# Expert blocks of four chunks on one resident x, and chunk states updated in pairs

## The chip, the cores and the metric

The kernel runs on one core of a Trainium2 chip. The metric is the time of one execution in microseconds of device time, as the median of several runs; one further execution was profiled, and all rows below come from it. Engines are named as in the profile: PE is TensorE, PEld its weight loads, DVE VectorE, ACT ScalarE, POOL GpSimd, SP the queue that issues the DMAs.

## The reference, cut to what matters

A gated linear attention (4 batches, 8 heads, 768 positions, head size 40) feeds a bilinear expert layer (3072 tokens, 320 to 1536 to 320).

```python
for t in range(S):                                   # per batch and head
    m_new = maximum(f_gate[t] + m, i_gate[t])
    f_stab, i_stab = exp(f_gate[t] + m - m_new), exp(i_gate[t] - m_new)
    C = f_stab * C + i_stab * outer(v[t], k[t])
    n = f_stab * n + i_stab * k[t]
    y[t] = sigmoid(o_gate[t]) * (C @ q[t]) / maximum(abs(n @ q[t]), 1)
x = y.transpose(0, 2, 1, 3).reshape(3072, 320)
out = ((x @ w_a) * (x @ w_b)) @ w_out
```

## The kernel before, in words

**Chunks.** The attention is computed in 24 chunks of 128 positions of one batch, in the order of `chunks`: chunk n belongs to batch n % 4 and to position group c = n // 4. A chunk's state (C and n, eight heads) goes to the chunk four places later. The chunk's stages are generators: `stage_e` (decay table `gbc`), `stage_a` (q and k split into bf16 parts `qks` and transposed into `T` by DMA), `stage_v` (v split), `stage_b` (scores, `pS`), `stage_i` (what the state gives, `pI`), `stage_c` (scores times v, `pV`, and the weighted v `vw` for the state), `stage_u` (state update: `pU`, `cst`, its bf16 split `cb`), `stage_f` (denominator and output gate, result y in `osig`) and `stage_d` (y transposed by PE into `pX`, then split into a high part `xh` and a low part `xl`: the expert layer's x). `put_state` and `get_state` carry the split state through device memory (`c_dram`) into the layout `cx` in which `stage_i` reads it. Chunks 0 to 5 take float32 forms (`begin_*`), the later ones bf16 splits. q, k and v lie in a ring of three chunks.

**Blocks.** `moe_block` runs the expert layer over a block of chunks: `sizes` is 2, 2, 3, 3, 3, 3, 3, 2, 3. For each of 12 slices of 128 hidden columns, `up` does two groups of 8 matmuls with the weights as stationary and x (256 or 384 columns) as moving operand into a PSUM bank `pu` each; the first group is copied out (`g`), the second multiplied with it (`g` again, on DVE), and the product is split into `gh` and `gl`; `down`, two slices behind (`LAG = 2`), does three matmuls of 320 columns for each chunk into the chunk's bank `pd`. After the last slice each `pd` is copied to `o` and stored.

**Order.** While block kb runs on the experts, the attention of block kb+1 runs beside it (`run_block`). Everything is first recorded in a `Plan`, which links the recorded nodes by their data and buffers, gives each a cost (`cost`), and settles by list scheduling in `TURNS` tries which engine does a free choice (`copier`: ACT or DVE; `adder`: DVE or POOL) and in which order each engine's and SP's in-order queue runs (`settle`). So all instructions are recorded with the same helper line, and the groups below are told apart by their tiles.

**Memory.** PSUM's eight banks are three for `pu` (shared with the early stages), three for `pd` and two for the attention (`ps_at`). `xh` and `xl` exist twice, so a block's x is written while the block before reads its own. Weights are converted early from 64-bit inputs through a ring `cv` of four buffers, which later takes the output tiles `o`.

Of the kernel before, what the change touches and what calls it, by code (L numbers as in the profile page):

```python
# [20 lines left out]
PSUM = bass.MemoryType.PSUM  # L21
TURNS = 40
TRIALS = 4
# [71 lines left out]
class Root:  # L95

    def __init__(self, make, ring, ndim, shape):
        self.make, self.tile, self.ring = make, None, ring
        self.full = tuple((0, n) for n in shape)
        self.first, self.users = None, []  # L100

# [6 lines left out]
class Node:  # L108
    __slots__ = ("i", "eng", "alts", "calls", "by", "prev", "next", "table", "acc", "wide", "use", "pair", "least")

    def __init__(self, i, alts):
        self.i, self.alts, self.eng = i, alts, alts[0]
        self.calls, self.prev, self.next, self.acc = [], {}, [], []
        self.by = {e: [0.0, 0.0, 0.0, False] for e in alts}
        self.table, self.wide, self.use = None, True, 0.0


class Plan:
# [20 lines left out]
    def add(self, engines, op, args, kw):  # L139
# [3 lines left out]
        acc = []  # L143
        for j, x in enumerate(refs):
            key, box = self.where(x)
            if key is not None:
                acc.append((key, box, j == 0))
                if j == 0 and op == "matmul" and not kw.get("start", True):
                    acc.append((key, box, False))
# [3 lines left out]
        if not (  # L153
            alts[0] == "PE" and node is not None and node.eng == "PE" and len(node.calls) < 8
            and (node.acc[0][0] == okey or self.pair and node.pair)
        ):
# [24 lines left out]
    def cost(self, node, by, eng, op, out, refs, args, kw):  # L181
# [5 lines left out]
        if eng == "PE":  # L187
            if op == "transpose":
                occ = 0.109
            else:  # L190
# [12 lines left out]
            by[1] = 0.17  # L203
            plain = size[1] == 4 and op == "matmul" and "float32r" not in f32[0]
            node.use += cols * refs[1].shape[0] * (1 + plain) / 128.0 * out.shape[0] / 128.0
# [78 lines left out]
    def run(self, rank, forward=True, fixed=None, odds=None):  # L284
# [17 lines left out]
        other = {"DVE": "POOL", "POOL": "DVE"}  # L302
        order, count, filling = [], 0, False

# [53 lines left out]
        while count < len(nodes):  # L358
# [56 lines left out]
            if e == "PE" and forward:  # L415
# [6 lines left out]
                while filling and fixed is None:  # L422
# [130 lines left out]
def kernel(  # L553
# [20 lines left out]
    DV = D + 2  # L574
    TB = 3
    NTB = TB * P
    WCH = 384
    CVB = 4
    STAGES = 8
# [18 lines left out]
    ps_at = tile_pool("ps_at", 2, PSUM)  # L598


    ident = wpool.tile([P, P], F32, name="ident")
# [15 lines left out]

    cst = [wpool.tile([P, HH, DV], F32, name=f"cst{b}") for b in range(B)]
    cxp = [[wpool.tile([P, H, DV], BF16, name=f"cx{b}_{w}") for w in range(2)] for b in range(B)]
# [34 lines left out]
    NCH = len(chunks)  # L654
    sizes = [2, 2, 3, 3, 3, 3, 3, 2, 3]
    NB = len(sizes)
# [380 lines left out]
    def stage_c(n):  # L1037
# [4 lines left out]
        if c < NC - 1:  # L1042
            vw = apool.tile([P, H, DV], F32, tag="vw", name=f"vw{n}", bufs=1)
            nc.gpsimd.tensor_tensor(
# [20 lines left out]

    def stage_u(n):
        c, b = chunks[n]
        if c == NC - 1:
            return
        s = st[n]  # L1070
# [4 lines left out]
        pu = pU[:, 0:HH * DV].rearrange("p (h d) -> p h d", h=HH)  # L1075
        for h in range(H):
            r, _, x = half(h)
            nc.tensor.matmul(
                pu[r:r + 64, x], nat(n)[0][:, 1, h, :], s["vw"][:, h], start=True, stop=True
            )  # L1080
        t = cst[b]
        if c == 0:
            nc.scalar.copy(t, pu)
        else:
            nc.vector.tensor_tensor(
                t, t, dec[:, c - 1, b * HH:(b + 1) * HH].unsqueeze(2).broadcast_to([P, HH, DV]),
                op=ALU.mult,
            )
            nc.vector.tensor_tensor(t, pu, t, op=ALU.add)
        yield  # L1090
        if n + B < NF32:
            return
        cb = apool.tile([P, 3, HH, DV], BF16, tag="cb", name=f"cb{n}", bufs=1)
        cr = apool.tile([P, H * DV], F32, tag="tmp", name=f"cr{n}")[:, 0:HH * DV]
        cr = cr.rearrange("t (h d) -> t h d", h=HH)
        nc.scalar.copy(cb[:, 2], t)
        nc.gpsimd.tensor_tensor(cr, t, cb[:, 2], op=ALU.subtract)
        yield
        if n < 8:
            nc.scalar.copy(cb[:, 1], cr)  # L1100
        else:
            nc.vector.tensor_copy(cb[:, 1], cr)
        nc.gpsimd.tensor_tensor(cb[:, 0], cr, cb[:, 1], op=ALU.subtract)
        states[n] = cb
        yield

# [42 lines left out]

    xt = {}  # L1150

    def stage_d(n):
        s = st[n] if n < NS else st.pop(n)
        k_ = block[n]
        t0 = (n - begins[k_]) * P
        if t0 == 0:
            xt[k_] = (
                mpool.tile([P, 3, NTB], F32R, tag="xh", name=f"xh{k_}", bufs=2),
                mpool.tile([P, 3, NTB], F32R, tag="xl", name=f"xl{k_}", bufs=2),
            )  # L1160
        xh, xl = xt[k_]
        pX = ps_at.tile([P, 512], F32, tag="pat", name=f"pX{n}")
# [9 lines left out]
        )  # L1172
        yield ("done", n)

# [4 lines left out]
    def aside(o, n):  # L1179
        if o == "L" and n + 2 < NCH and n + 2 > NS + 1:  # L1180
            load(n + 2)
        if o == "P":
            put_state(n - 1)
        if o == "G" and NE < n + 2 < NCH:
            load_g(n + 2)
        if o == "C":
            get_state(n - 1)
        if o == "O" and n % B == 0 and n > 0:
            load_o(n // B)

    def early_chunk(n):
# [3 lines left out]
        aside("P", n)  # L1195
        if n > NS:
            yield from stage_d(n - 1)
# [13 lines left out]
    def late_chunk(n):  # L1211
        parts = {
            "b": stage_b(n, 0), "B": stage_b(n, 1), "i": stage_i(n), "d": stage_d(n - 1),
            "c": stage_c(n), "u": stage_u(n), "f": stage_f(n),
        }
        if n + 1 < NCH:
            parts |= {"e": stage_e(n + 1), "a": stage_a(n + 1), "v": stage_v(n + 1)}
        for o in PATTERN:
            if o in parts:
                x = next(parts[o], "end")  # L1220
                if x != "end":
                    yield x
            else:
                aside(o, n)
# [3 lines left out]
    def attention():  # L1228
        for n in range(NS, NCH):
            yield from (early_chunk if n < NF32 else late_chunk)(n)  # L1230
        yield from stage_d(NCH - 1)


    def moe_block(kb):
        NT = sizes[kb] * P
        xh, xl = (x[..., 0:NT] for x in xt.pop(kb))
        pd = [ps_dn.tile([P, 512], F32, tag=f"pd{t}", name=f"pd{kb}_{t}") for t in range(sizes[kb])]
        gs = {}

        def down(ff):  # L1240
            need(STAGES * (ff // 3) + 6 + ff % 3)
            gh, gl = gs.pop(ff)
            for t in range(sizes[kb]):
                cols = slice(t * P, (t + 1) * P)
                wh, wl = w_down(ff)
# [16 lines left out]
        def up(ff):  # L1262
            need(STAGES * (ff // 3) + 5)
            acc = [
                ps_up.tile([P, NTB], F32, tag="pu", name=f"pu{kb}_{ff}_{j}")[:, 0:NT]
                for j in range(2)
            ]
            for j in range(2):
                terms = []
                for kt in range(2):  # L1270
                    h, l = w_up(ff, kt, j)
                    terms += [(h, xh[:, kt, :]), (h, xl[:, kt, :]), (l, xh[:, kt, :])]

                h = w_up(ff, 2, j)
                terms += [(h, xh[:, 2, :]), (h, xl[:, 2, :])]
                for x, (a, r) in enumerate(terms):
# [24 lines left out]
    def begin_e(n):  # L1301
# [5 lines left out]
        for hf in range(2):  # L1307
            pE = ps_up.tile([P, HH, P], F32, tag="pu", name=f"pE{n}_{hf}")
            for x in range(HH):
# [7 lines left out]
    def begin_a(n):  # L1317
# [6 lines left out]
        for j in range(2):  # L1324
# [5 lines left out]
            T.append(t)  # L1330
            pool, tag = (ps_at, "pat") if n >= NS or n + j == 0 else (ps_up, "pu")
            pT = pool.tile([P, 512], F32, tag=tag, name=f"pT{n}_{j}")
            pt = pT.rearrange("p (h t) -> p h t", h=HH)
# [50 lines left out]
    def weigh(n):  # L1384

        c, b = chunks[n]
        vw = apool.tile([P, H, DV], F32, tag="vw", name=f"vw{n}", bufs=1)
        nc.gpsimd.tensor_tensor(
# [33 lines left out]
    cpool = tile_pool("cpool", 1)  # L1422
    mpool = tile_pool("mpool", 3)

    def run(g, times=1):
# [99 lines left out]
    def rest():  # L1525
# [7 lines left out]
        for n in range(NS):  # L1533
            weigh(n)
            yield from stage_u(n)
            if n == 0:
                load(NS + 1)
        squash(0, NS, B - NS)
# [4 lines left out]
    def run_block(kb):  # L1543
# [55 lines left out]
```

## Time and profile before

| what | value |
|---|---|
| median of 3 runs | 534.09 us (533.82 to 535.54) |
| the profiled execution | 534.12 us, its span 532.3 us |
| instructions in the span | 12505, of them 4862 matmuls |
| busy: PE, DVE, ACT, POOL | 523.2, 411.4, 236.3, 147.9 us |
| granted TensorE clock, mean | 0.994 |
| DMA | 66.77 MB moved, mean 125 GB/s |

Busy times are sums over the span; a matmul's end is modelled and overlaps the next matmul's start, so a busy PE says only that work was there. How long a stream of matmuls takes is read from start to start: a row of the chain of waits that merges 16 matmuls gives 16 such steps. In a timeline row the first number is the start in us from the span's start, the second the time to the end of the row's last instruction, and the bracket the engine's idle time before it with the one that ended it.

### The profile page before, as it was taken

Reading aid. Unit: us, or ns where it says so; the run is one execution under the profiler, and the core shown is the slowest. Engines: PE = TensorE matmul, PEld = TensorE weight load, DVE = VectorE, ACT = ScalarE, POOL = GpSimd, SP = SyncE. Lnnn points to the kernel's source line nnn. Section 1 sums busy time; section 2 is a strip of 40 time slices with the busy share of each in tenths; the row PEclk is TensorE's granted clock in tenths of the full one; section 3 lists DMA queues with packets and bytes.
Section 4 is the critical chain, followed back from the end, with each engine's and each line's share of the span. In section 5 each row is a group of like instructions: output and inputs, shape, how many; then the busy total and the mean of one; then the engine's idle time right before and its main releaser. Section 6 shows DMA issues by size and latency. Waiting matters only on the chain.

```text
span 532.3 us, 12505 instructions
## 1 busy us (share of the span) xinstructions
PE 523.2 (98%) x4862; PEld 497.1 (93%) x4862; DVE 411.4 (77%) x919; ACT 236.3 (44%) x568; POOL 147.9 (28%) x194
## 2 busy tenths in 40 slices
PE   8889999999999999999999999999999999999997
PEld 6679999999999999999999999999999999999997
DVE  5999999799979859888599776888489848843332
ACT  5759997543456142346243344543215515212111
POOL 2015134414326505534223423526050301000000
PEclk9899999999999999999999999999999999999999
DMA  9998866978696864886755766765537427000001
GB/s 172 305 245 182 238 167 135 137 148 165 117 188 129 148 146 104 155 158 104 169 105 97 158 119 157 155 99 114 130 73 140 93 41 156 2 1 25 2 1 37
DMA packets 198679, 66.77 MB, mean 125 GB/s; under 512 B 184252, under 2 KB 191900, under 8 KB 198620
## 3 DMA queue, kind: packets, MB, share of 16 engines
q1 hardware_dynamic: 198620, 65.98, 59.6%
q8 instruction: 38, 0.62, 0.5%
q14 instruction: 21, 0.17, 0.1%
HBM read 41.11 MB, written 5.97 MB: 88 GB/s over the span
## 4 chain that ended last, share of the span: by engine, by line
PE 81%; DVE 7%; issue 3%; DMA 2%; ACT 2%; SPq 1%; POOL 0%; ACTq 0%; DVEq 0%; POOLq 0%
PE pu L522 46%; PE pd L522 22%; PE pV L522 4%; PE pS L522 3%; PE pU L522 2%; DVE qks L522 2%; DVE w L522 2%; PE pI L522 2%; SPq L522 1%; PE pX L522 1%; DMA qk<-in_k_dram 1%; DVE cw L522 1%; DMA gbc<-g_dram 1%; DMA c_dram<-cb 1%; DVE osig L522 1%
## 5 line engine op out<-in xcount | busy, mean ns | idle before, releaser
L522 PE MATMUL pu<-xh,w 128*128 128x384 f32 (+1 forms) x1080 | 277.2, 325 | 0.1
L522 PE MATMUL pu<-xl,w 128*128 128x384 f32 (+1 forms) x648 | 203.9, 323 | 0.9 <-DVE xl L522 0.9
L522 PEld LDWEIGHTS pu<-xh,w 128*128 128x128 f32 x1080 | 190.0, 189 | 1.7 <-ACT xh L522 0.6
L522 PE MATMUL pd<-w,gh 128*128 128x320 f32 x576 | 135.1, 315 | 0.3 <-ACT gh L522 0.2
L522 PEld LDWEIGHTS pu<-xl,w 128*128 128x128 f32 x648 | 121.1, 189 | 1.4 <-DVE xl L522 1.2
L522 PEld LDWEIGHTS pd<-w,gh 128*128 128x128 f32 x576 | 97.0, 188 | 1.0 <-ACT gh L522 0.7
L522 DVE TENSOR_TENSOR g<-pu,g 128x384 f32<-128x384 f32 (+1 forms) x108 | 54.6, 506 | 53.4 <-PE pu L522 50.2
L522 ACT COPY g<-pu 128x384 f32<-128x384 f32 (+1 forms) x99 | 43.7, 442 | 113.8 <-PE pu L522 112.6
L522 PE MATMUL pd<-w,gl 128*128 128x320 f32 x288 | 86.6, 310 | 0.1
L522 ACT ACTIVATE gbc<-gbc,gtab 128x128 f32<-128x128 f32 x160 | 52.7, 394 | 3.3 <-POOL gbc L522 3.3
L522 PEld LDWEIGHTS pd<-w,gl 128*128 128x128 f32 x288 | 53.4, 188 | 0.3 <-DVE gl L522 0.3
L522 POOL TENSOR_TENSOR gl<-g,gh 128x384 fp32r<-128x384 f32 (+1 forms) x24 | 26.4, 1102 | 81.4 <-ACT gh L522 46.0
L522 DVE TENSOR_TENSOR gl<-g,gh 128x384 fp32r<-128x384 f32 (+1 forms) x84 | 46.4, 553 | 2.1 <-DVE gh L522 0.5
L522 ACT CAST gh<-g 128x384 fp32r<-128x384 f32 (+1 forms) x44 | 20.5, 465 | 39.9 <-DVE g L522 39.8
L522 DVE TENSOR_TENSOR gbc<-pS,gbc 128x512 f32<-128x512 f32 x48 | 32.6, 681 | 4.7 <-ACT gbc L522 3.7
L522 POOL TENSOR_TENSOR vr<-va 128x336 f32<-128x336 f32 x18 | 14.0, 775 | 79.0 <-PE pV L522 71.1
L522 PE MATMUL pV<-va,gbc 128*128 128x42 bf16 (+1 forms) x240 | 34.5, 221 | 0.0
L522 POOL TENSOR_TENSOR vw<-va,gtab 128x336 f32<-128x336 f32 x20 | 16.2, 808 | 64.9 <-PE pU L522 58.1
L522 PEld LDWEIGHTS <-T 120*128 120x128 bf16 x576 | 25.4, 97 | 7.6 <-issue 5.1
L522 DVE TENSOR_TENSOR gbc<-gbc,pb 128x512 f32<-128x512 f32 x36 | 29.4, 817 | 0.4 <-ACT pb L522 0.3
L522 DVE TENSOR_TENSOR pb<-gbc 128x512 bf16<-128x512 f32 x36 | 29.0, 806 | 0.3
L522 POOL TENSOR_SCALAR_AFFINE_SELECT gbc<-gbc 128x1024 f32<-128x1024 f32 x20 | 25.0, 1248 | 11.7 <-DMA gbc<-g_dram 11.7
(109 smaller groups left out, 768.7 us busy)
## 6 DMA issues: line engine op xcount, KB each, us to landing
gbc<-g_dram SPq DMA_DIRECT2D x20, 512.0 KB
qk<-in_q_dram SPq DMA_DIRECT2D x24, 160.0 KB
qk<-in_k_dram SPq DMA_DIRECT2D x24, 160.0 KB
va<-in_v_dram SPq DMA_DIRECT2D x24, 160.0 KB
osig<-in_o_gate_dram SPq DMA_DIRECT2D x24, 160.0 KB
raw<-in_moe_w_out_dram SPq DMA_DIRECT2D x12, 320.0 KB
out_dram<-o SPq DMA_DIRECT2D x24, 160.0 KB
raw<-in_moe_w_a_dram SPq DMA_DIRECT2D x8, 384.0 KB
```

The costliest lines, as they stand in the source:

```text
L522: f(*[real(x) for x in args], **{k: real(x) for k, x in kw.items()})
```

## The change

It does these things together:

- The blocks become 2, 2, 4, 4, 4, 4, 4 chunks: seven instead of nine. An `up` matmul of a block of four has 512 moving columns.
- `xh` and `xl` exist once, with four chunk slots. A block's chunks take the slots of the block before, except that block 1 has slots 2 and 3, and block 2's first two chunks the slots 0 and 1, which are free by then. Where a slot is still read by the block before (`later`), `stage_d` of the chunk is recorded behind that block's experts.
- PSUM becomes two banks for `pu`, four for `pd`, two for the attention. In blocks of two, and in the early stages, `up_bank` takes the idle fourth `pd` bank every third time, so there are three banks there.
- Odd chunks update the state of their pair: `stage_u(n)` does nothing for even n, and for odd n the 16 state matmuls of both chunks, as one node, and one update, copy and split over twice the columns. `vw` has two buffers for that. The k tile of the chunk two places on goes into the slot of the pair's first chunk, so its load is recorded behind the pair's update, apart from the q load.
- `put_state` and `get_state` of both chunks of a pair follow in the next chunk.
- The ring `cv`, and with it `o` in blocks after the first, has three buffers instead of four.
- The planner takes 80 tries instead of 40, a slightly changed price of an `up` or `down` matmul, a price of 0.12 us where PE goes between full matmuls and those with few rows or output partitions, and sees x chunk by chunk (`grain`).

```diff
-TURNS = 40
+TURNS = 80
...
-                    occ = cols / 2400 + 0.0135
+                    occ = cols / 2400 + 0.0105 + 0.0000125 * cols
...
+                if x.mode != mode:
+                    t += 0.12
+                    mode = x.mode
...
-    TB = 3
+    TB = 4
+    NSL = 4
-    CVB = 4
+    CVB = 3
...
-    ps_up = tile_pool("ps_up", 3, PSUM)
+    ps_up = tile_pool("ps_up", 2, PSUM)
...
+    def up_bank(shape, name, few=True):
+        turn[0] += 1
+        if few and turn[0] % 3 == 0:
+            return ps_dn.tile(shape, F32, tag="pd3", name=name)
+        return ps_up.tile(shape, F32, tag="pu", name=name)
...
-    sizes = [2, 2, 3, 3, 3, 3, 3, 2, 3]
+    sizes = [2, 2, 4, 4, 4, 4, 4]
...
     def stage_u(n):
         c, b = chunks[n]
-        if c == NC - 1:
+        if c == NC - 1 or n % 2 == 0:
             return
...
+        plan.pair = True
+        for j, m in enumerate((n - 1, n)):
+            for h in range(H):
+                r, _, x = half(h)
+                nc.tensor.matmul(
+                    pu[r:r + 64, j * HH + x], nat(m)[0][:, 1, h, :], st[m]["vw"][:, h],
+                    start=True, stop=True,
+                )
+        plan.pair = False
+        t = cst2[b // 2]
...
+        if n > NS and n + 2 < NCH:
+            load_qk(n + 2, (1,))
...
+    slots = [list(range(x)) for x in sizes]
+    slots[1] = [2, 3]
+    for x in range(3, NB):
+        slots[x] = [0, 1, 2, 3]
+    slots[NB - 1] = slots[NB - 1][0:sizes[NB - 1]]
...
+    def later(n):
+        k_ = block[n]
+        return k_ > 1 and slot(n) in slots[k_ - 1]
...
+    xh, xl = (mpool.tile([P, 3, NSL * P], F32R, tag=f"x{w}", name=f"x{w}", bufs=1) for w in "hl")
+    xh.root.grain = xl.root.grain = P
...
             done = r is not None and r[1] >= last
+        for n in range(begins[kb + 1], begins[min(kb + 2, NB)]):
+            if later(n):
+                run(stage_d(n), 4)
```

More of the change, by code (lines that the diff above doesn't have):

```diff
@@ L99, in __init__ @@
         self.full = tuple((0, n) for n in shape)
-        self.first, self.users = None, []
+        self.first, self.users, self.grain = None, [], None
     def get(self):
@@ L108 @@
 class Node:
-    __slots__ = ("i", "eng", "alts", "calls", "by", "prev", "next", "table", "acc", "wide", "use", "pair", "least")
+    __slots__ = ("i", "eng", "alts", "calls", "by", "prev", "next", "table", "acc", "wide", "use", "pair", "least", "mode")
     def __init__(self, i, alts):
@@ L114, in __init__ @@
         self.by = {e: [0.0, 0.0, 0.0, False] for e in alts}
-        self.table, self.wide, self.use = None, True, 0.0
+        self.table, self.wide, self.use, self.mode = None, True, 0.0, 0
 class Plan:
@@ L146, in add @@
             if key is not None:
-                acc.append((key, box, j == 0))
+                g = key.grain if isinstance(key, Root) else None
+                p, q = box[-1]
+                for u in range(p, q, g or q - p):
+                    acc.append((key, box[:-1] + ((u, min(u + (g or q), q)),), j == 0))
                 if j == 0 and op == "matmul" and not kw.get("start", True):
@@ L153, in add @@
         if not (
-            alts[0] == "PE" and node is not None and node.eng == "PE" and len(node.calls) < 8
+            alts[0] == "PE" and node is not None and node.eng == "PE" and len(node.calls) < (16 if self.pair else 8)
             and (node.acc[0][0] == okey or self.pair and node.pair)
@@ L203, in cost @@
             by[1] = 0.17
+            node.mode = 1 if refs[1].shape[0] <= 64 else 2 if out.shape[0] <= 64 else 0
             plain = size[1] == 4 and op == "matmul" and "float32r" not in f32[0]
@@ L302, in run @@
         other = {"DVE": "POOL", "POOL": "DVE"}
-        order, count, filling = [], 0, False
+        order, count, filling, mode = [], 0, False, 0
         def put(x, r):
@@ L616 @@
     HH = H // 2
-    cst = [wpool.tile([P, HH, DV], F32, name=f"cst{b}") for b in range(B)]
+    cst2 = [wpool.tile([P, 2 * HH, DV], F32, name=f"cst{b}") for b in range(B // 2)]
+    cst = [cst2[b // 2][:, b % 2 * HH:(b % 2 + 1) * HH] for b in range(B)]
     cxp = [[wpool.tile([P, H, DV], BF16, name=f"cx{b}_{w}") for w in range(2)] for b in range(B)]
@@ L1074, in stage_u @@
             pU = ps_at.tile([P, 512], F32, tag="pat", name=f"pU{n}")
[L1075 to L1081, printed above, removed]
+        pu = pU[:, 0:H * DV].rearrange("p (h d) -> p h d", h=H)
+        plan.pair = True
[8 more added lines that the diff above has]
+        t = cst2[b // 2]
         if c == 0:
@@ L1090, in stage_u @@
         yield
[L1091 to L1105, printed above, removed]
+        if n + B >= NF32:
+            cb = apool.tile([P, 3, H, DV], BF16, tag="cb", name=f"cb{n}", bufs=1)
+            cr = apool.tile([P, H * DV], F32, tag="tmp", name=f"cr{n}")
+            cr = cr.rearrange("t (h d) -> t h d", h=H)
+            nc.scalar.copy(cb[:, 2], t)
+            nc.adder.tensor_tensor(cr, t, cb[:, 2], op=ALU.subtract)
+            yield
+            nc.copier.copy(cb[:, 1], cr)
+            nc.adder.tensor_tensor(cb[:, 0], cr, cb[:, 1], op=ALU.subtract)
+            states[n - 1], states[n] = cb[:, :, 0:HH], cb[:, :, HH:]
+            yield
+        if n > NS and n + 2 < NCH:
+            load_qk(n + 2, (1,))
     states = {}
@@ L1148, in stage_f, with slot, inner @@
         yield
-    xt = {}
-    def stage_d(n):
[L1153 to L1161, printed above, removed]
+    slots = [list(range(x)) for x in sizes]
[3 more added lines that the diff above has]
+    slots[NB - 1] = slots[NB - 1][0:sizes[NB - 1]]
+    def slot(n):
+        return slots[block[n]][n - begins[block[n]]]
+    def later(n):
+        k_ = block[n]
+        return k_ > 1 and slot(n) in slots[k_ - 1]
+    def inner(n):
+        return n >= NS and block[n] == block[n + 1] and not later(n)
+    def stage_d(n):
+        s = st[n]
+        t0 = slot(n) * P
         pX = ps_at.tile([P, 512], F32, tag="pat", name=f"pX{n}")
@@ L1172, in stage_d @@
         )
-        yield ("done", n)
+        yield
     PATTERN = "LbababPaBaBaBaiaaGvdvdCedOeeececfufuu"
@@ L1180, in aside @@
         if o == "L" and n + 2 < NCH and n + 2 > NS + 1:
-            load(n + 2)
+            whole = n % 2 == 0 or chunks[n][0] == NC - 1
+            load_qk(n + 2, (0, 1) if whole else (0,))
+            load_v(n + 2)
         if o == "P":
+            put_state(n - 2)
             put_state(n - 1)
@@ L1186, in aside @@
         if o == "C":
+            get_state(n - 2)
             get_state(n - 1)
@@ L1195, in early_chunk @@
         aside("P", n)
-        if n > NS:
+        if inner(n - 1):
             yield from stage_d(n - 1)
@@ L1212, in late_chunk @@
         parts = {
-            "b": stage_b(n, 0), "B": stage_b(n, 1), "i": stage_i(n), "d": stage_d(n - 1),
+            "b": stage_b(n, 0), "B": stage_b(n, 1), "i": stage_i(n),
             "c": stage_c(n), "u": stage_u(n), "f": stage_f(n),
         }
+        if inner(n - 1):
+            parts["d"] = stage_d(n - 1)
         if n + 1 < NCH:
@@ L1222, in late_chunk @@
                     yield x
-            else:
+            elif o != "d":
                 aside(o, n)
@@ L1230, in attention @@
             yield from (early_chunk if n < NF32 else late_chunk)(n)
-        yield from stage_d(NCH - 1)
+            if n + 1 == begins[block[n] + 1]:
+                if not later(n):
+                    yield from stage_d(n)
+                yield ("done", n)
     def moe_block(kb):
         NT = sizes[kb] * P
-        xh, xl = (x[..., 0:NT] for x in xt.pop(kb))
+        base = min(slots[kb])
+        xs = [x[..., base * P:base * P + NT] for x in (xh, xl)]
         pd = [ps_dn.tile([P, 512], F32, tag=f"pd{t}", name=f"pd{kb}_{t}") for t in range(sizes[kb])]
@@ L1243, in down @@
             for t in range(sizes[kb]):
-                cols = slice(t * P, (t + 1) * P)
+                cols = slice((slots[kb][t] - base) * P, (slots[kb][t] - base + 1) * P)
                 wh, wl = w_down(ff)
@@ L1264, in up @@
             acc = [
-                ps_up.tile([P, NTB], F32, tag="pu", name=f"pu{kb}_{ff}_{j}")[:, 0:NT]
+                up_bank([P, NTB], f"pu{kb}_{ff}_{j}", sizes[kb] < 4)[:, 0:NT]
                 for j in range(2)
@@ L1307, in begin_e @@
         for hf in range(2):
-            pE = ps_up.tile([P, HH, P], F32, tag="pu", name=f"pE{n}_{hf}")
+            pE = up_bank([P, HH, P], f"pE{n}_{hf}")
             for x in range(HH):
@@ L1330, in begin_a @@
             T.append(t)
-            pool, tag = (ps_at, "pat") if n >= NS or n + j == 0 else (ps_up, "pu")
-            pT = pool.tile([P, 512], F32, tag=tag, name=f"pT{n}_{j}")
+            if n >= NS or n + j == 0:
+                pT = ps_at.tile([P, 512], F32, tag="pat", name=f"pT{n}_{j}")
+            else:
+                pT = up_bank([P, 512], f"pT{n}_{j}")
             pt = pT.rearrange("p (h t) -> p h t", h=HH)
@@ L1386, in weigh @@
         c, b = chunks[n]
-        vw = apool.tile([P, H, DV], F32, tag="vw", name=f"vw{n}", bufs=1)
+        vw = apool.tile([P, H, DV], F32, tag="vw", name=f"vw{n}", bufs=2)
         nc.gpsimd.tensor_tensor(
@@ L1536, in rest @@
             if n == 0:
-                load(NS + 1)
+                load_qk(NS + 1, (0,))
+                load_v(NS + 1)
+            else:
+                load_qk(NS + 1, (1,))
         squash(0, NS, B - NS)
```

10 lines of the change are left out of this document (5 added, 5 removed).

## The prediction, made before the changed kernel was run

> **What bounds the kernel now.** I read the head of the page first, then the chain of waits, then the busy time by windows cut where the blocks change.
>
> ```profile
> span 532.3 us, 12505 instructions
> PE 523.2 (98%) x4862; PEld 497.1 (93%) x4862; DVE 411.4 (77%) x919; ACT 236.3 (44%) x568; POOL 147.9 (28%) x194
> ```
> ```profile
> core 0: us, PE busy (x) PEld busy (x) DVE busy (x) ACT busy (x) POOL busy (x), PEclk, DMA share, GB/s
> 40.00:88.00 48.00, 47.67 (x452) 45.01 (x449) 46.15 (x107) 45.22 (x113) 18.85 (x27) 1.00 0.76 178
> 88.00:135.00 47.00, 46.55 (x508) 44.87 (x507) 42.84 (x109) 23.73 (x62) 15.61 (x20) 1.00 0.85 156
> 196.00:257.00 61.00, 61.00 (x594) 58.12 (x593) 50.45 (x106) 25.44 (x62) 24.36 (x29) 1.00 0.70 135
> 480.00:529.10 49.10, 49.07 (x299) 48.80 (x297) 17.72 (x36) 7.16 (x16) 0.00 (x0) 1.00 0.02 8
> ```
>
> PE has work without a break from about 40 us to the end, at a granted clock of 1.00 in each of these windows. The windows are, in order: most of block 0, block 1, a block of three with attention beside it, the last block alone. DVE is at 96% and 91% in the first two and at 83% in the middle, so the start is where a second engine is nearly as tight as PE. What a busy PE achieves is read from starts, in the chain of waits:
>
> ```profile
> 191.94 3.95 PE pd L522 x27
> 469.57 1.92 PE pu L522 x16
> 479.73 8.32 PE pu L522 x48
> 497.61 2.80 PE pu L522 x16
> ```
>
> 16 matmuls of 256 columns take 1.92 us (120 ns each), 48 of 384 columns 8.32 and 16 of them 2.80 us (173 to 175 ns, I take 174), 27 of 320 columns 3.95 us (146 to 147 ns). A block of three alone is 12 x 16 x 0.174 + 12 x 9 x 0.147 = 49.3 us, and the last block's window is 49.1 us long. A middle block takes 61 us, so three chunks' attention add 12 us of PE. No slack is left there: time goes down only by fewer or cheaper PE steps, and goes up with every new wait of PE.
>
> **The up matmuls.** From 256 to 384 columns a step grows by 54 ns for 128 columns; another 128 make 174 + 54 = 228 ns. The columns multiplied stay the same, so what goes is the part of a step that doesn't scale: 120 - 2 x 54 = 12 ns. Before, six blocks of three and three of two: 6 x 192 x 0.174 + 3 x 192 x 0.120 = 200.4 + 69.1 = 269.5 us. After: 5 x 192 x 0.228 + 2 x 192 x 0.120 = 218.9 + 46.1 = 265.0 us. That is -4.5 us, for 384 matmuls fewer. Bounds: a step in proportion to the columns (232 ns) would give -0.7; with 173 ns for today's step, and so 226 for the wide one, it is -5.3. The Trainium skill, "TensorE: Matmul & The Clock Gate", section Back-to-back issue gap, gives a warm gap of the columns over 2.4 GHz plus 2.5 ns; by it the 384 matmuls saved would be worth only 1 us. The rows disagree: they show 120 and 174 ns where that formula gives 109 and 162.
>
> The down matmuls keep their number (864) and their 320 columns: nothing.
>
> **The state matmuls.** They work on 64 output partitions, and PE pays for going there and back:
>
> ```profile
> 342.42 0.34 PE L522 MATMUL pu<-xh,w 128*128 128x384 f32 x1
> 342.69 0.67 PE L522 MATMUL pU<-vw,qk 128*64 128x42 f32 x16
> 343.28 0.44 PE L522 MATMUL pu<-xl,w 128*128 128x384 f32 x1
> 343.56 0.51 PE L522 MATMUL pu<-xh,w 128*128 128x384 f32 x2
> ```
>
> The step ahead of the group is 0.27 instead of 0.174 us, the group 0.59, the step behind it 0.28: 0.10 + 0.59 + 0.11 = 0.80 us for one chunk's 16 records. There are 20 such groups, and 10 remain with 32 records. The entry and the exit (0.21) surely go; at most half the interruption (0.40) is fixed. I take 0.3: -3.0 us (bounds -2.1 to -4.0). On DVE, ACT and POOL the pair's update, casts and differences are half as many at twice the size; those engines are not the bound after the second block, so nothing.
>
> **Two banks for pu.** A bank's next group may start when the copy or product has read it. Before:
>
> ```profile
> L522 DVE TENSOR_TENSOR g<-pu,g 128x384 f32<-128x384 f32 x72 | 39.6, 550 | 44.3 <-PE pu L522 43.5 <-ACT cb L522 0.4 <-issue 0.3
> L522 DVE TENSOR_TENSOR g<-pu,g 128x256 f32<-128x256 f32 x36 | 15.0, 417 | 9.1 <-PE pu L522 6.7 <-issue 1.8 <-ACT g L522 0.3
> L522 ACT CAST xh<-pX 128x384 fp32r<-128x384 f32 x24 | 11.4, 473 | 11.6 <-PE pX L522 11.4
> L522 DVE TENSOR_TENSOR xl<-pX,xh 128x384 fp32r<-128x384 f32 x24 | 13.3, 552 | 2.5 <-ACT xh L522 2.3
> ```
>
> The product grows from 550 to 550 + 133 = 683 ns. One slice of a block of four takes PE 16 x 0.228 + 12 x 0.147 + 16/12 (four chunks' attention, 4 us each) = 6.7 us, of which the bank's own group is 1.8: 4.9 us remain for a product of 0.7 us, and 3.6 us in the last block, where no attention stands beside it. The wait today runs the other way: DVE idles 43.5 us because it is early for `pu`. I take 0. If DVE's queue held the product back by over 4 us, PE would wait; that is a rival below.
>
> **One x.** The x of the next block can be written only after the last `up` group of this one. Per chunk three transposes, 0.473 us of ACT, 0.552 us of DVE; the DVE part of four chunks is 2.2 us, to which the last slice's product, gh and gl add some 1.8, and the first copy and a few hand-overs 1: about 5 us. PE has cover: the 36 down matmuls of the last three slices (36 x 0.147 = 5.3 us; today's 27 are the 3.95 us row above), the 12 transposes (1.3 us) and what the next attention chunk offers. Block 1 hands over only two chunks and has 18 x 0.147 = 2.6 us of cover. I take 0.2 us for each of the five hand-overs, +1.0 us; without cover they would be 5 x 2 = 10 us; it cannot be under 0.
>
> **The start.** This is where work moves. Before, block 2 needs the x of chunks 4 to 6; now it needs chunk 7 too, while PE has only the same two blocks of two to run meanwhile.
>
> ```profile
> 131.66 0.44 PE pd L522 x3
> 132.10 0.33 PE pX L522 x3
> 133.31 0.62 PE pV L522 x24
> 133.92 0.60 PE pU L522 x16
> 135.15 0.89 PE pu L522 x5
> ```
> ```profile
> 132.98 0.56 DVE L522 TENSOR_TENSOR xl<-pX,xh 128x384 fp32r<-128x384 f32 x1 [0.18 <-ACT xh L522]
> 133.91 0.69 DVE L522 TENSOR_TENSOR pb<-gbc 128x512 bf16<-128x512 f32 x1
> 138.65 0.50 DVE L522 TENSOR_TENSOR num<-pV,num 128x336 f32<-128x336 f32 x1
> 142.03 0.49 DVE L522 TENSOR_TENSOR osig<-num,osig 128x320 f32<-128x320 f32 x1
> 150.83 0.54 DVE L522 TENSOR_TENSOR xl<-pX,xh 128x384 fp32r<-128x384 f32 x1
> ```
>
> Chunk 6's x is complete at 133.5, block 2's first group starts at 135.2, when block 1's last down matmuls have just run out. Chunk 7's y is ready at 142.5 and its x at 151.4, but unhurried: between 133.9 and 142.5 DVE also splits q and k of chunk 8 and serves block 2. Chunk 7's own DVE work after 133.5 is the rest of pb 0.69, num 0.50, three small den steps (0.5), two osig products (1.0) and xl 0.55: 3.2 us, with PE and ACT steps and hand-overs between them some 5 us. So its x can be there at 138.5. PE has for that time the rest of pV, pX and what it saved before, about nothing net: a wait of some 3 us. DVE's 9% idle time (4.2 us) and ACT's half in the window 88 to 135 could take more; for the other end, x at 151.4 as today, less the 4 us of attention work that PE then does meanwhile, gives 12. I take +3 (0 to 12), nearest to the hurried count, since a free list schedule will hurry it.
>
> **The rest.** SP: k of an odd chunk is loaded after the pair's update instead of at its chunk's head, and eight state stores come in a row instead of four. The longest such load on the chain shows its price:
>
> ```profile
> 97.52 4.38 DMA qk<-in_k_dram
> ```
>
> It is needed a chunk later (a middle chunk takes 20 us), the states three chunks later, so both are hidden; without that lead 4.4 us would show each time. POOL's `vw` gets a second buffer; POOL is busy for 28% of the span, so that gives nothing. `osig` has one buffer, so the next gates load only after a block's four transposes; the first result that needs them is a chunk away. The tail:
>
> ```profile
> 527.78 0.87 ACT L522 COPY o<-pd 128x320 f32<-128x320 f32 x2 [3.98 <-PE pd L522]
> 528.24 1.70 SPq L522 DMA_DIRECT2D out_dram<-o  x3
> 529.15 0.43 ACT L522 COPY o<-pd 128x320 f32<-128x320 f32 x1 [0.50 <-PE pd L522]
> ```
>
> With four outputs and three buffers the fourth copy waits until the first store has landed. Steps of 0.44 us per chunk put the first store's issue 0.8 us before PE's end. The last store here needs at most 2.7 us from its issue to the span's end; if it all counted, +1.9, if the first landed in time 0; I take +0.7, as the span's end holds more than the landing. More tries and new prices of the planner: what order can still win are PE's remaining waits, which the windows put at some 1 us after 40; a new order can lose as much, so 0 (-1 to +1).
>
> **Sum.** Against the profiled execution's 534.12 us (span 532.3 and 1.8 around it; the median of the runs, 534.09, is the same): -4.5 - 3.0 + 1.0 + 3.0 + 0.7 = -2.8, so 531.3 us.
>
> **Rivals.**
> - *The start costs nothing* (the planner takes the spare DVE and ACT time, hand-overs are covered): -7.5 + 0.7, so 527.3. For it: ACT's half-idle window. Against: DVE at 96% before 88 us.
> - *The start starves PE* (the other side): chunk 7's x comes as late as today, +12 instead of +3: 540.3. It decides from 7.5 us of wait on, where the savings are used up. For it: DVE's 96 and 91%. Against: only 3.2 us of DVE work are truly needed.
> - *Two banks are too few*: PE waits on `pu`. 5 blocks x 12 slices x 2 groups = 120 hand-overs; 0.05 us each, +6: 537.3. It needs a product held back by over 4 us in DVE's queue, and DVE shows 43.5 us of being early. The Trainium skill, "Perfetto Trace Analysis", section Matmuls, says independent groups should rotate through banks so that evacuation overlaps the next group; by that, three are better than two, and this trace shows only that two engines reach three banks in time.
> - *The hand-over of x isn't covered*: 5 x 1 us more, 536; it would show as PE idle before each block's first group.
> - *A wide matmul brings nothing*: step 232 ns, +3.8, so 535.1. Against it: the steps of 120 and 174 ns. The gap formula of the Trainium skill, "TensorE: Matmul & The Clock Gate", section Back-to-back issue gap, would end close by, with -1.0 for the up matmuls: 534.8.
>
> **How the numbers follow.** About 0.3% (1.6 us) is what can be told from no change. Chances: the forecast (529 to 532.8) 0.43, the cheap start (526 to 529) 0.16, the starved start 0.13, two banks 0.08, the hand-over 0.12, no gain from width 0.08. Faster: 0.41 of the first and all of the second, 0.57. Same: 0.02, half of the hand-over and most of the width, 0.16. Slower: the rest, 0.27. The range leaves out the far part of the starved start and of the best case: 526.5 to 537.5. The likeliest case alone is 529 to 532.8.
>
> **What would show it.** 16 `up` matmuls of 512 columns in a row take 3.65 us in the chain; ten groups of 32 state records; the copy of the fourth `o` starts over 1 us after PE's end; PE idle before block 2's first group of 0 to 6 us. The prediction is wrong if PE shows waits on `pu` within blocks or on `xl` at each boundary, or if block 2 starts after 143.

## The result: slower by 1.3%, and the profile after

The changed kernel's median is 541.36 us (540.62 to 542.23), against 534.42 us for the kernel before beside it: ratio 1.0128 (95%: 1.0103 to 1.0153), 6.9 us slower. The forecast was 531.3 us and a range up to 537.5. The profiled execution of the changed kernel took 540.88 us, 6.8 us more than that of before; the readings below compare these two. First the head of its page, which answers to the first fence of the prediction:

```profile
span 539.1 us, 11543 instructions
PE 525.0 (97%) x4491; PEld 451.1 (84%) x4491; DVE 414.6 (77%) x870; ACT 225.3 (42%) x512; POOL 116.2 (22%) x149
```

371 matmuls fewer are recorded, and PE is still busy for 1.8 us more. Next the windows of the changed kernel, cut at PE's first expert matmul (28.2), at about block 1's start, at block 2's first group and at PE's end, with one middle block and the last block by themselves:

```profile
core 0: us, PE busy (x) PEld busy (x) DVE busy (x) ACT busy (x) POOL busy (x), PEclk, DMA share, GB/s
28.20:85.40 57.20, 55.22 (x524) 51.75 (x523) 55.86 (x125) 50.01 (x116) 16.60 (x24) 1.00 0.86 209
85.40:138.20 52.80, 50.53 (x569) 48.02 (x568) 49.83 (x119) 28.94 (x76) 16.85 (x20) 1.00 0.83 147
138.20:535.80 397.60, 393.48 (x3197) 331.40 (x3194) 287.86 (x579) 129.47 (x287) 77.46 (x80) 1.00 0.51 101
224.30:306.50 82.20, 82.20 (x736) 69.28 (x733) 66.93 (x141) 32.32 (x73) 21.33 (x23) 1.00 0.72 142
469.80:535.80 66.00, 66.00 (x337) 57.07 (x336) 22.22 (x37) 9.08 (x17) 0.00 (x0) 1.00 0.04 15
```

The same three cuts in the trace of before:

```profile
23.30:85.00 61.70, 60.09 (x559) 55.54 (x560) 59.25 (x130) 52.75 (x126) 20.03 (x30) 0.96 0.84 205
85.00:135.00 50.00, 49.42 (x524) 47.22 (x523) 45.84 (x117) 26.19 (x70) 16.65 (x21) 1.00 0.82 151
135.00:529.10 394.10, 394.07 (x3616) 379.75 (x3614) 289.71 (x629) 141.87 (x343) 107.62 (x122) 1.00 0.52 103
```

The window less PE's busy time is PE's idle time. After block 2's start it was 0.03 us and is 4.12 us. Block 2 starts at 138.2 instead of 135.0, as forecast. From there to PE's end it takes 3.5 us more, although chunk 7's attention now lies ahead of that point. The granted clock is 1.00 in both. What PE achieves is read from the chain of waits, in the changed kernel's last block:

```profile
469.92 11.20 PE pu L529 x48
482.44 3.73 PE pu L529 x16
486.17 1.76 PE pd L529 x12
487.94 3.73 PE pu L529 x16
```

16 steps of 512 columns take 3.73 us, 48 take 11.20: 233 ns each, not 228. 12 steps of 320 columns take 1.76 us (147 ns), as before. The waits of PE in the changed kernel (total, times, longest, us):

```profile
PE pu L529 <- DVE g L529: 1.6, 2, 1.1
PE pI L529 <- DVE gbc L529: 1.3, 1, 1.3
PE pX L529 <- DVE osig L529: 1.2, 2, 0.6
PE warm L529 <- DVE idle L529: 1.2, 1, 1.2
PE pu L529 <- ACT g L529: 1.1, 1, 1.1
PE pX L529 <- DVE xl L529: 1.0, 1, 1.0
```

Waits on `pu` within blocks are the sign that the prediction named for its own failure, and there are three (2.7 us). The timeline gives the place of one:

```profile
349.57 0.31 PE L529 MATMUL pd<-w,gl 128*128 128x320 f32 x1
351.00 0.50 PE L529 MATMUL pu<-xh,w 128*128 128x512 f32 x1 [1.13 <-ACT g L529]
371.00 0.48 PE L529 MATMUL pu<-xl,w 128*128 128x512 f32 x1
371.41 1.13 PE L529 MATMUL pU<-vw,qk 128*64 128x42 f32 x32
372.47 0.56 PE L529 MATMUL pd<-w,gh 128*128 128x320 f32 x2
```

The first two rows show a `pu` group that stands still until ACT's copy `g` is done. The other three are a state group of 32 records, of which there are ten, as forecast. Last the tail:

```profile
532.40 0.43 ACT L529 COPY o<-pd 128x320 f32<-128x320 f32 x1 [4.41 <-PE pd L529]
535.92 0.43 ACT L529 COPY o<-pd 128x320 f32<-128x320 f32 x1 [0.50 <-PE pd L529]
```

The last copy starts 0.1 us behind PE's end (535.8), not over 1 us: the order ended chunk 0's `pd` 3.5 us early, and the fourth buffer that is missing cost nothing.

### The profile page after: what moved, and what is told of

Its sections match the earlier page's. It is cut to its first block, busy times and chain, and to the rows that moved or that the text cites. A ratio compares the mean times of both kernels' runs of the same rounds, so it can differ in the third digit from the quotient of the medians.

```text
span 539.1 us, 11543 instructions
## 1 busy us (share of the span) xinstructions
PE 525.0 (97%) x4491; PEld 451.1 (84%) x4491; DVE 414.6 (77%) x870; ACT 225.3 (42%) x512; POOL 116.2 (22%) x149
## 4 chain that ended last, share of the span: by engine, by line
PE 71%; DVE 14%; DMA 5%; ACT 3%; SPq 2%; issue 2%; POOL 0%; DVEq 0%; ACTq 0%
PE pu L529 40%; PE pd L529 19%; DVE qks L529 5%; PE pV L529 4%; PE pS L529 3%; DVE gbc L529 2%; DMA qk<-in_k_dram 2%; PE pU L529 2%; SPq L529 2%; DVE pb L529 2%; PE pI L529 1%; DMA c_dram<-cb 1%; DVE osig L529 1%; DVE g L529 1%; PE pX L529 1%
## 5 line engine op out<-in xcount | busy, mean ns | idle before, releaser
L529 PE MATMUL pu<-xh,w 128*128 128x512 f32 (+1 forms) x840 | 254.2, 370 | 3.2 <-DVE g L529 1.6
L529 PE MATMUL pu<-xl,w 128*128 128x512 f32 (+1 forms) x504 | 180.7, 366 | 0.0
L529 PEld LDWEIGHTS pu<-xh,w 128*128 128x128 f32 x840 | 149.3, 188 | 25.6 <-DVE g L529 2.9
L529 PEld LDWEIGHTS pu<-xl,w 128*128 128x128 f32 x504 | 94.1, 188 | 11.9 <-DVE xl L529 0.3
L529 ACT COPY g<-pu 128x512 f32<-128x512 f32 (+1 forms) x75 | 39.9, 532 | 150.8 <-PE pu L529 148.8
L529 DVE TENSOR_TENSOR g<-pu,g 128x512 f32<-128x512 f32 (+1 forms) x84 | 51.2, 609 | 65.6 <-PE pu L529 64.7
L529 DVE TENSOR_TENSOR gl<-g,gh 128x512 fp32r<-128x512 f32 (+1 forms) x71 | 48.0, 676 | 1.8
L529 ACT CAST gh<-g 128x512 fp32r<-128x512 f32 (+1 forms) x37 | 19.3, 521 | 33.3 <-DVE g L529 33.1
L529 PEld LDWEIGHTS <-pb 128*128 128x128 bf16 x576 | 25.0, 96 | 8.2 <-issue 5.5
L529 PE MATMUL pV<-va,pb 128*128 128x42 bf16 x288 | 28.2, 183 | 0.4 <-DVE pb L529 0.4
```

What stands on the lines that cost most here:

```text
L529: f(*[real(x) for x in args], **{k: real(x) for k, x in kw.items()})
```

## The experiments

Every ratio is against the kernel before beside it, with its 95% interval.

### The parts alone

**Two banks.** The kernel before with one `pu` bank fewer:

```diff
-    ps_up = tile_pool("ps_up", 3, PSUM)
+    ps_up = tile_pool("ps_up", 2, PSUM)
```

> The kernel before with two PSUM banks for pu instead of three, and one bank left unused; blocks of three as before. Theory that two banks cost PE waits on the copies and products: 2 to 6 us longer (536 to 540), with PE idle before pu, released by DVE or ACT g. Rival, that three against two make nothing and the waits of the changed kernel are only its order: within 1 us of the kernel before.

535.74 us, 1.0027 (1.0015 to 1.0038), 1.4 us and so between the two expectations.

**Paired states alone.** Before's blocks, with the state update in pairs, two buffers of `vw`, the k load behind the pair, and a ring `cv` of three. For room, the small table `ends` moves into an unused part of another tile.

```diff
+        if c == NC - 1 or n % 2 == 0:
...
-        t = cst[b]
+        t = cst2[b // 2]
...
-    CVB = 4
+    CVB = 3
```

> The kernel before with the states of two chunks updated together (and the later k load and the three buffers of cv that go with it), blocks of three, x twice and three pu banks kept. Theory: the ten state groups fewer give 2.7 us of PE and nothing takes it back: 531 to 532. Rival, that the odd chunk's k load and the bursts of state stores stand on the path: at or over 534.

536.58 us, 1.0032 (1.0011 to 1.0053). The expected gain did not come; the time is the rival's, but the order is another one here too, so this run does not show that the k load or the stores cost it.

**Blocks of four alone.** The changed kernel with before's `stage_u`, states and loads:

```diff
-        if c == NC - 1 or n % 2 == 0:
+        if c == NC - 1:
...
-        t = cst2[b // 2]
+        t = cst[b]
```

> The changed kernel with each chunk's state updated singly again; blocks of four, one x and the new PSUM shares kept. Theory, that the blocks of four carry the loss and the pairs are a gain of 2.7 us: 543 to 545. Rival, that the pairs with the k load behind them made the loss: 535 or less.

531.90 us, 0.9953 (0.9937 to 0.9969). The theory, that the blocks carry the loss, is refuted for this order; the time is close to the 531.3 us that were forecast for the whole change, which other draws below do not repeat. Its chain has:

```profile
474.29 3.65 PE pu L529 x16
477.94 1.75 PE pd L529 x12
479.69 3.65 PE pu L529 x16
```

The very same matmul takes 228 ns here and 233 in the changed kernel. Neither its size nor its neighbours differ.

### The step by itself

**Widths.** A stream of `up` steps alone, in float32r with the weights changed each time and no other engine at work; no part of the reference is computed.

```diff
+        for n in (256, 320, 384, 448, 480, 512):
+            section(n, pa)          # 64 steps, groups of 8, two banks
+        section(512, one)           # one bank
+        section(512, tri)           # three banks
+        section(512, alt, each=True)
```

> Only a stream of the up matmuls' kind (float32r, 128x128 weights changed every time, groups of 8 into a PSUM bank), 64 of each width, with nothing else beside them; no part of the reference is computed. Theory: the step at 512 columns is 233 ns even here, against 120, 147 and 174 at 256, 320 and 384, so the cost that does not scale grows from 12 to 20 ns by itself, somewhere above 384. Rival: alone the step at 512 is 226 to 228, and the 233 in the changed kernel come from what runs beside it or from its PSUM banks. If one bank, three banks or two accumulators in turn change the step at 512, it is the bank; if not, the width.

The windows of 64 steps of 256, 448 and 512 columns:

```profile
18.07:25.93 7.86, 7.86 (x66) 7.83 (x65) 0.00 (x0) 0.00 (x0) 1.00 0.01 2
46.42:59.64 13.22, 13.22 (x65) 12.02 (x65) 0.00 (x0) 0.00 (x0) 1.00 0.00 0
73.51:88.06 14.55, 14.55 (x65) 12.02 (x64) 0.49 (x1) 0.00 (x0) 1.00 0.02 6
```

They give 123, 207 and 227 ns (the first with its start; 120 from step to step). One, two or three banks make no difference:

```profile
88.06 14.67 PE L45 MATMUL one<-x,w 128*128 128x512 f32 x64
102.57 14.67 PE L45 MATMUL tri<-x,w 128*128 128x512 f32 x64
117.07 14.67 PE L45 MATMUL alt<-x,w 128*128 128x512 f32 x64
```

The rows start 14.5 us apart, 227 ns a step. So 228 was the right price for the matmul; something in the changed kernel adds 5 ns.

**Places.** The two kernels' `up` differ in one thing that no instruction shows: the address of x in SBUF. In the built programs x and the expert weights lie a multiple of 256 bytes apart in the kernel before and in the blocks alone, and 32 bytes off such a multiple in the changed kernel. A stream puts four copies of x at 0, 32, 64 and 96 bytes off the weights `we`, and other weights `wg` 64 off; no part of the reference is computed.

```diff
+    xe = big("xe")
+    pad("pada", 4)
+    xf = big("xf")
+    pad("padb", 4)
+    xg = big("xg")
+    wg = weights("wg")
+    pad("padc", 4)
+    xh = big("xh")
```

> Only a stream of the up matmuls' kind as in the stream of widths, with the moving operand x at four places in SBUF against one place of the weights: xe at the same offset within 64 bytes as the weights we, xf 32 bytes off it, xg 64 bytes on, xh 96 bytes on; 256, 320, 384 and 512 columns each, and then 512 columns with weights wg. No part of the reference is computed. Theory: where x and the weights lie 32 bytes apart within 64 (xf, xh), the step is that of the changed kernel, 117, 147, 174 and 233 ns; where they agree (xe, xg), it is 120, 147, 173 and 227. Rival: the place makes nothing, all four show 227 at 512 columns.

Windows of 64 steps of 512 columns: four copies at 0, 32, 64 and 96 against `we`, then the first copy against `wg`, so 192, and the third, so 0.

```profile
45.30:59.85 14.55, 14.55 (x66) 12.02 (x65) 0.00 (x0) 0.00 (x0) 1.00 0.00 0
88.01:102.94 14.93, 14.93 (x65) 12.00 (x65) 0.00 (x0) 0.00 (x0) 1.00 0.00 0
130.67:145.32 14.65, 14.65 (x65) 12.03 (x65) 0.00 (x0) 0.00 (x0) 1.00 0.00 0
173.68:188.61 14.93, 14.93 (x66) 12.02 (x65) 0.00 (x0) 0.00 (x0) 1.00 0.00 0
188.61:203.54 14.93, 14.93 (x65) 11.97 (x64) 0.00 (x0) 0.00 (x0) 1.00 0.00 1
203.54:218.04 14.50, 14.50 (x65) 11.82 (x63) 0.49 (x1) 0.00 (x0) 1.00 0.01 5
```

14.55 and 14.50 us are 227 ns, 14.93 us is 233, 14.65 us 229. The slow copies are slow with the same data, banks and neighbours. The first copy is fast against `we` and slow against `wg`, and `wg` is fast with the third copy: what counts is the distance of x from the weights.

### The place of x in the kernel

**Shifts of 96 and of 480 bytes.** Each of the three buffers of `cv` is made longer by 32 or by 160 bytes, which moves x and, behind it, `gh` and `gl`. The planner's order stays, instruction by instruction.

```diff
-            cpool.tile([P, WCH], ...
+            cpool.tile([P, WCH + 8], ...     # 96 bytes in all; WCH + 40: 480
```

> The changed kernel with 32 bytes more in each of the three buffers of cv, so that x, gh and gl lie 32 bytes further on; every engine's instructions and their order are the same. Theory, that the 233 ns of its wide step come from the place of x against the weights: the step falls to 227 to 229, 960 of them make 4 to 5.5 us, 536 to 538. Rival, that they come from what runs beside: within 1 us of the changed kernel's 541.4.

> The changed kernel with 160 bytes more in each of the three buffers of cv, 480 in all, so that x lies a multiple of 256 bytes from the weights, as in the kernel before and in the one without pairs; instructions and order are those of the changed kernel. The shift by 96 bytes brought nothing, since in the stream of places the step was 227 only where x and weights agree within 256 bytes. Theory: the wide step falls from 233 to 227, 5 us less, 536 to 537. Rival, that the place acts only in a bare stream: 541.

With 96 bytes 541.33 us, 1.0116 (1.0095 to 1.0136): no gain. Distance 128 is a slow one too (232.4 ns a step in this trace); I had taken the rule to repeat every 64 bytes. With 480 bytes the distance is 0 modulo 256, and the time 538.68 us, 1.0068 (1.0047 to 1.0089). The chain of the kernel with 480 bytes:

```profile
493.80 3.65 PE pu L529 x16
504.64 3.65 PE pu L529 x16
```

The mean step, between `up` neighbours without a wait, goes from 232.8 to 229.1 ns; 960 of them make 3.5 us. By the ratios it is 0.6%, 3.2 us (some 1.7 us either way), less than the 5 expected. From block 2's start to PE's end the traces show 397.6 us for the changed kernel, 397.5 with 96 bytes and 394.2 with 480. No instruction differs, and a shift that leaves the distance bad brings nothing, so this part of the loss is shown to be the place. The steps of `down`, whose stationary operands `gh` and `gl` move too, go from 147.5 to 146.8 ns, 0.6 us in all, so most of it is x.

### The order

Of the other 3.7 us, the first suspect was the k load, which stands on the changed kernel's chain ahead of block 2:

```profile
95.47 1.06 PE pU L529 x32
97.05 4.09 DMA qk<-in_k_dram
101.16 0.47 ACT qks L529
```

**Single updates for chunks 0 to 7**, k loaded early as before:

```diff
+        if n < SINGLE:              # SINGLE = 8
+            yield from single_u(n)
+            return
```

> The changed kernel with the states of chunks 0 to 7 updated singly, and the k tiles loaded with q as before up to chunk 9; pairs from chunk 8 on; x where the changed kernel has it. Theory, that the pairs hurt by the k load of chunk 7 that waits for the pair of 4 and 5: block 2 starts at 135 to 137 instead of 138, 2 to 3 us less, 538 to 540. Rival, that the pairs hurt in the long middle by worse order (more waits and more changes between attention and experts on PE): within 1 us of 541.4.

538.74 us, 1.0074 (1.0046 to 1.0101). But block 2 started at 141.5, later than the 138.2 it was to improve on; the gain lies behind it. The planner had made another order throughout, so this run says nothing of the load. That raised the question of what an order is worth by itself. The planner draws noise for its tries from a generator with seed 7. Another seed changes nothing but the order of the queues and the free choices of engine.

**Other draws.** The seed (11, 13, 17) in the kernel before, in the changed kernel, and in the changed kernel with x shifted by 480 bytes. For the blocks alone seed 11 gave the very order of seed 7, so there the start ranks get noise instead.

```diff
-        rng = np.random.default_rng(7)
+        rng = np.random.default_rng(11)
```
```diff
-        rank, base, best = [float(x.i) for x in self.nodes], None, None
+        rank, base, best = [x.i + rng.normal(0.0, 1.0) for x in self.nodes], None, None
```

> The changed kernel with another seed of the planner's tries, nothing else. Theory, that some of the loss is the luck of one order: the time moves by 1 to 4 us either way, the waits of PE lie at other places. Rival, that the structure sets the waits: within 1 us of 541.4, waits of the same sum.

> The changed kernel with the other seed and x at a multiple of 256 bytes from the weights: both gains add up, 528.5 to 530, if place and order act apart. Rival, that the order's gain lay in the same steps: 533 to 534.

> The kernel before with the other seed of the planner's tries, nothing else. Theory, that any order of this planner is good or bad by some us: 533 to 540, most likely slower than 534.5. Rival, that the kernel before is steady against the seed and only the changed one is not: within 1 us of 534.5.

> The blocks of four without the pairs (531.9 with the first seed) with the other seed. Theory, that its gain is the structure's: 530 to 534. Rival, that it was the luck of one order: 535 or more.

> The kernel before with the third seed. Theory, that the kernel before runs a good order among orders that differ by some us: 534 to 539. Rival, that its orders differ little: 534 to 535.5.

> As the kernel before with the third seed, with a fourth: 534 to 539, or 534 to 535.5 by the rival.

> The changed kernel with x a multiple of 256 bytes from the weights and a third seed. Theory, that the change in itself gains a few us and the first seed's order was a bad draw: 528 to 535. Rival, that the second seed's order was the lucky one and the change in itself loses: 536 or more.

> As the one with the third seed, with a fourth: 528 to 535, or 536 or more by the rival.

> Blocks of four without the pairs, with the planner started from a slightly shuffled order (another seed alone had left its order as it was, and so only repeated the 531.9). Theory, that blocks of four gain in themselves and the pairs take it back: 531 to 535, and from block 2's first up matmul to PE's end 386 to 389 us. Rival, that 531.9 was one lucky order: 536 or more, and 391 us or more.

> As the other shuffled start, with another shuffle: 531 to 535 and 386 to 389 us, or by the rival 536 or more and 391 us or more.

| kernel | seed 7 | 11 | 13 | 17 | mean |
|---|---|---|---|---|---|
| before | 1 | 1.0033 (1.0020 to 1.0045) | 1.0103 (1.0087 to 1.0118) | 1.0034 (1.0021 to 1.0048) | 1.0043 |
| changed | 1.0128 (1.0103 to 1.0153) | 0.9986 (0.9975 to 0.9997) | | | |
| changed, x + 480 bytes | 1.0068 (1.0047 to 1.0089) | 0.9927 (0.9915 to 0.9939) | 1.0063 (1.0046 to 1.0080) | 1.0042 (1.0022 to 1.0063) | 1.0025 |
| blocks alone | 0.9953 (0.9937 to 0.9969) | 1.0046 (1.0016 to 1.0076), noise | 0.9999 (0.9983 to 1.0015), noise | | 1.0000 |

(The repeat of the blocks alone with seed 11 gave 0.9956, 0.9944 to 0.9968.) One seed moves the changed kernel by 7.1 us, and the kernel before by up to 5.5. The order that before ships with is the best of its four; the changed kernel's, with x in place, is the slowest of its four, hardly worse than that of seed 13. With seed 11 and x in its place the time is 530.75 us, 0.7% faster than before with its own seed. That is close to the forecast, but it took the best of four draws. The place is worth the same there (0.9986 to 0.9927, 3.2 us).

Not all of this was expected. Seed 11 moves the changed kernel by more than 1 to 4 us, and seed 13 brings the kernel before above 539. Place and seed add up, but to 530.75 us instead of 530 or less. Both further draws of the placed kernel fall to the rival (536 or more), and so does one of the two shuffled starts of the blocks alone (536.69 us, the other 534.57). Head and waits of the fastest kernel, with seed 11 and x in its place:

```profile
span 529.0 us, 11527 instructions
PE 517.4 (98%) x4489; PEld 449.8 (85%) x4489; DVE 411.8 (78%) x866; ACT 219.5 (41%) x505; POOL 126.7 (24%) x160
```
```profile
PE pX L529 <- DVE osig L529: 2.5, 2, 2.2
PE warm L529 <- DVE idle L529: 1.2, 1, 1.2
PE pu L529 <- DVE g L529: 1.0, 1, 1.0
```

It has the same two banks, one x and paired states, and of 2.7 us of waits on `pu` 1.0 is left, all of it ahead of block 2: PE idles for 0.84 us behind its start. So another order alone removes those waits. Whether three banks would remove the rest isn't shown: behind block 2's start before's four orders, with three banks, leave PE no gaps, and the four placed ones, with two banks and one x, 0.8 to 4.4 us.

## Why the prediction was wrong

The 6.9 us come apart by the ratios of the table:

| part | us |
|---|---|
| place of x (1.0128 to 1.0068) | +3.2 |
| the changed kernel's order against the mean of its four (1.0068 to 1.0025) | +2.3 |
| before's order against the mean of its four (1 to 1.0043) | +2.3 |
| the change itself, mean to mean | -0.9 |

The first line is shown by a pair of kernels that differ in nothing else. The others rest on four draws each, which spread by 0.43% and 0.66% (standard deviation): the change itself is -0.9 us with a standard error of about 2.1 us, so whether it gains anything by itself, or the forecast 2.8 us, stays open. Without seed 7 on either side it is -2.5 us, and no surer. The planner's new prices and its 80 tries are part of the change in every changed kernel; what they do to the orders wasn't tested.

Where it sits in the trace is told by PE's time from each matmul's start to the next, summed by kind, with true gaps apart (us, each trace's own time):

| | before | changed | x + 480 | x + 480, seed 11 | blocks alone |
|---|---|---|---|---|---|
| first `up` starts at | 23.3 | 28.2 | 29.8 | 25.1 | 22.8 |
| `up` | 282.5 | 279.8 | 277.5 | 276.2 | 276.5 |
| `down` | 131.4 | 134.9 | 134.3 | 134.0 | 134.2 |
| state | 12.0 | 10.7 | 10.7 | 10.7 | 12.0 |
| attention | 77.5 | 73.7 | 73.6 | 75.2 | 75.8 |
| idle | 2.2 | 8.4 | 9.1 | 4.3 | 4.8 |

By the prediction's own steps:

- **"The up matmuls ... That is -4.5 us": the first step that failed.** The price of 228 ns was right for the matmul (227 alone, 228 in the blocks alone) and wrong for this program: x fell on a bad address, a cost that the prediction did not have. By the traces' mean steps between `up` neighbours without a wait, the `up` matmuls cost 1152 x 0.1755 + 576 x 0.1193 = 270.9 us before and 960 x 0.2328 + 384 x 0.1173 = 268.5 us in the changed kernel, which is -2.4 instead of -4.5. With x in its place (0.2291 and 0.1193) they cost 265.7 us, -5.2. The step of the rival *A wide matmul brings nothing*, 232 ns, came true by a mechanism that the rival didn't have. The formula in the Trainium skill, "TensorE: Matmul & The Clock Gate", section Back-to-back issue gap, which is for the gap of an isolated matmul, gives 216 ns at 512 columns; the streams show 227 and 233.
- **"a new order can lose as much, so 0 (-1 to +1)": the second.** The spread of orders is not 1 us but 5 to 8 (534.4 to 539.8 for before, 530.75 to 538.7 for the changed kernel with x in place). The prediction looked only at PE's remaining waits of the one order in the profile, 0.03 us after block 2's start, and so took a well-drawn order for the normal one. This is the larger part of the miss: seed 11, with nothing else changed, takes 7.1 us from the changed kernel. With seed 13 before's own span grows from 532.3 to 538.2 us.
- **"The down matmuls keep their number (864) and their 320 columns: nothing"**: the step stays at 147 ns, but the kind takes 3.5 us more. An expert step right behind attention or state matmuls takes some 85 ns longer, there are 167 such steps instead of 150, and with fewer `up` steps more of them fall on `down`: 74 instead of 47, some 2.3 us of the 3.5. `up` and `down` together save 3.4 us on the mean of the four placed kernels against before's four, in which the state groups' entries and exits are included.
- **State matmuls, -3.0**: right within its bounds. Group by group, with entry and exit, they cost 2.4 us less (14.7 to 12.3); without them 1.3 (table). Alone, in the kernel with pairs, this gain did not show in the time.
- **The start, +3**: the number is right, the mechanism isn't shown. Block 2 starts at 138.2 instead of 135.0, and the means over the draws, 139.2 and 136.6, differ by 2.6. But PE doesn't wait for chunk 7's x: in the 9 us ahead of block 2 it idles for 0.1 us. The delay is there from the first expert matmul on (28.2 instead of 23.3); from it to block 2's start the changed kernel takes 110.0 us, 1.7 less than before. What delays that first matmul stays open, so the number counts as luck.
- **One x, +1.0**: right in size. In this order it shows as the one wait of `pX` on `xl`, 1.0 us, at one hand-over instead of 0.2 us at each of five. The upper bound of 10 us counted 2 us a hand-over, where its own working has about 5 us of work to cover.
- **Two banks, 0**: not refuted. The waits on `pu` that the prediction named as a sign against it do appear, 2.7 us, but they go with another order. In the kernel before, one bank fewer gave +0.27%, no more than another draw of the same kernel. The rival *Two banks are too few* asked for +6. The rule in the Trainium skill, "Perfetto Trace Analysis", section Matmuls, that groups should rotate through banks so that evacuation overlaps the next group, is met by two banks with seed 11: behind block 2's start PE waits for `pu` once, for 0.06 us.
- **The tail, +0.7**: 0 (the rows above).
- **k of an odd chunk, "needed a chunk later"**: in the changed kernel it isn't; its load stands on the chain for 4.09 us. What it costs isn't shown, as the run that loaded it early had another order.

Paired states and blocks of four may also disturb each other: from block 2's start to PE's end the blocks alone take 388.8 us on the mean of three orders, the placed kernels with pairs 391.5 on four. The spreads overlap (386.6 to 390.2, 388.9 to 394.2), so this stays open as well.

## What to carry to other kernels

Where a planner with random tries makes the order, time several draws of both versions before a change gets the credit or the blame: here one draw was worth more than the change. After any change of a tile's size, look at where the operands of the hot matmuls have come to lie, since an unchanged instruction can get slower by its address alone. Price a matmul in a stream from start to start, and then look for the same row in the kernel itself.

## What the runs showed of the hardware

- A float32r matmul of 512 columns, with new weights each time, takes 227 ns when x lies a multiple of 256 bytes from the weights, 229 at 64 bytes off, and 233 at 32, 96 and 192. At 384 columns it is 173 against 177 ns, at 320 no difference (147), at 256 columns 113 to 120 with no such pattern. Other distances weren't measured alone; in the kernel a distance of 128 gives 232 at 512 columns, where 0 gives 229.
- With x at a multiple of 256 bytes from the weights, the step isn't linear in the columns: 120, 147, 173, 207, 217 and 227 ns at 256, 320, 384, 448, 480 and 512.
- Going back from attention matmuls to a float32r expert matmul costs some 85 ns on the first step: 231 instead of 147 ns at 320 columns, behind bf16 matmuls and float32 transposes alike.
